# Three chunks of rows asked for together ahead of a weight load, their halo copies on another queue, and one product moved

## The chip, the core and the metric

The kernel runs on one core of a Trainium2 chip. A core has a matrix engine (TensorE, PE in the profile), a vector engine (VectorE, DVE), a scalar engine (ScalarE, ACT), a general engine (GpSimd, POOL) and a queue engine (SyncE, SP). Each takes its own instructions in their order; semaphores make one wait for another. Transfers (DMA) are issued by an instruction on GpSimd's or SyncE's queue and run on 16 DMA engines. SBUF is the memory on the core, PSUM the small one that matmuls write. The metric is the time of one execution in microseconds (us).

## What is computed

For `x` of 8 batches, 4224 tokens and 192 channels:

```python
w = softmax(weight)                       # 8 heads, 7 taps
x = causal depthwise convolution of x with w
theta = x @ w_theta                       # 192 x 192
zr, zi = x * cos(theta), x * sin(theta)
y = w_tok_r @ zr + w_tok_i @ zi           # over tokens, each w_tok 4224 x 4224
u = x + y
out = u + relu(u @ w_ch)                  # 192 x 192
```

Nearly all of the work is in the two token mixes, which are matmuls of 4224 x 4224 by 4224 x 1536.

## The kernel before

**Tiles and steps.** The tokens are cut into 33 *chunks* of 128 (four runs of 32 tokens each, `token`, L140). For each chunk the convolution, the transposes, the *channel mix* with `w_theta` and the products with cos and sin give the right sides z; sums and differences of them serve a scheme in which two output tiles of 128 tokens take seven products for each chunk instead of eight. A *step* (class `Step`) computes such a pair of output tiles over the chunks that are active; there are 58 steps. A *product* is two matmuls (L603), one for each half of the columns, 384 wide. Steps 0 and 1 are `plain`: 8 products for each chunk, with 2 and 4 chunks, 16 and 32 products. Step 2 has 5 chunks and 35 products, step 3 has 7 chunks and 49. Counting on over steps, products 1 to 16 are step 0's, 17 to 48 step 1's, 49 to 83 step 2's, 84 to 132 step 3's.

The seven runs of a step (L507 to L513) are written "11", "S1", "S2", "S4", "S3", "12", "22". Each adds into one of the PSUM tiles c1, c2, c3 and ends by *giving* it to the partial rows `pv` (`give`, L482): a copy on ScalarE (L488) or an addition on VectorE (L490). `y` tiles come from a pool of two (L105, L597). In step 2 run "S4" ends with product 68 and gives by VectorE; run "12" opens c3 with product 74, while c1 is still in use.

**The first pass over chunks 0 to 11** is the loop at L900. Iteration i convolves chunk i (`conv`, L212, two halves; line 220 is the matmul, and each half reads 96 partitions of `xw`, first of tokens runs 0 and 1, then of 2 and 3), transposes it, and mixes chunk i-1 (`theta`, L284: eight matmuls at L150, then two Sin on ScalarE at L295; products with z at L301, sums at L310 on VectorE). In between, `between(n)` lets n products of the steps pass (`more`, L876). From iteration 4 on there are 11 products in an iteration: 2 behind the first half of the convolution, 1 behind the first channel mix, 2 behind the second half, 1 behind the second mix, and 5 more. Iteration 5 holds products 25 to 35, 6 holds 36 to 46, 7 holds 47 to 57, 8 holds 58 to 68, 9 holds 69 to 79, 10 holds 80 to 90. The results of the convolution, the mixes and the transposes share two PSUM buffers in turn (`banks`, L117).

**Events.** Each step has a list of events (`step_events`, L719) with a place between 0 and 7, a seventh of the step's products being one unit; at its place an event is written into the instruction streams. They hold the weights' transposes on VectorE (`turn`, L394, from `st` to `wt`), their sums and differences (`wsum`, L402), the weight loads of the step after the next (`load_w`, L376: four DMAs on GpSimd's queue into one of two `st` tiles, first for `w_tok_r`, "m=1", at 1.3, then for `w_tok_i`, "m=2", at 4.3) and `load_rows` of the next step at 1.6 (L443: it asks for the step's two `pv` tiles). A weight load needs the `st` tile whose last transpose has been read. Step 3's second weights are loaded in step 1 at 4.3, ahead of product 37; its transpose "22", the first that reads them, is written ahead of product 60.

**Rows.** `Chunk.__init__` (L190) fills `xw` with a chunk's rows: for each of four runs a DMA from `x` on GpSimd's queue (L207, with a cast to 16 bits), and 16 rows of *halo*, the rows before the run, copied out of the `xw` tile of the chunk before by a DMA on SyncE's queue (L198). A chunk's halo copies so need the rows of the chunk before. `xw` tiles share a pool of six buffers, tag "big", with the `pv` tiles of steps from 2 on (L192, L448). In the loop, `load_chunk(i + 3)` stands behind the second channel mix.

**What sets the order.** PE, VectorE and ScalarE take their instructions as written (`in_order`, L79). On GpSimd's queue the weight loads are chained among each other (`pool`, L94), the rows' loads are not; SyncE's DMAs are not chained. Where nothing is chained the framework orders an engine's instructions at compile time. SyncE also issues the stores of convolved rows (`store`, L263) and of partial rows at the end of a step (L616, two of 768 KB).

Of the kernel before, what the change touches and what calls it, by code (L numbers as in the profile page):

```python
# [16 lines left out]
def kernel(  # L17
# [23 lines left out]
    nc = tc.nc  # L41
# [8 lines left out]
    NQ = 4  # L50
    Q = P // NQ
    NK = S // P
    NT = S // P
    HALO = 16
    WR = Q + HALO
# [5 lines left out]
    NW = 11  # L61
# [26 lines left out]
    def dve(ins):  # L88
        return in_order("dve", ins)
# [4 lines left out]
    def pool(ins):  # L94
        return in_order("pool", ins)
# [39 lines left out]
    def channel_pieces(w):  # L135

        return ((slice(0, P), 0, w[0:P, :]), (slice(0, R), 1, w[P:D, :]),
                (slice(R, P), 2, w[0:R, :]), (slice(0, P), 3, w[R:D, :]))

    def token(k, a):  # L140

        return (a * NK + k) * Q
# [44 lines left out]
    class Chunk:  # L187


        def __init__(self, k, before=None):  # L190
            self.k = k
            self.xw = wk.tile([2 * WR, 2, B, D], F16, name="xw", tag="big", bufs=6)  # L192
            for a in range(NQ):
                h, lo = a // 2, (a % 2) * WR
                t0 = token(k, a)
                hist = self.xw[lo : lo + HALO, h, :, :]
                if before is not None:
                    nc.sync.dma_start(  # L198
                        out=hist, in_=before.xw[lo + Q : lo + Q + HALO, h, :, :]
                    )  # L200
                elif t0 == 0:
                    nc.vector.memset(hist, 0.0)
                else:
                    lo, t0 = lo - HALO, t0 - HALO
                lo += HALO
                n = (a % 2 + 1) * WR - lo
                nc.gpsimd.dma_start(  # L207
                    out=self.xw[lo : lo + n, h, :, :],
                    in_=x[:, t0 : t0 + n, :].rearrange("b s d -> s b d"),
                )  # L210

        def conv(self, j):  # L212
# [95 lines left out]
        def sum(self, o, a, b):  # L308
            z = self.z
            dve(nc.vector.tensor_tensor(  # L310
                out=z[:, o, :], in0=z[:, a, :], in1=z[:, b, :], op=ALU.subtract
            ))
# [18 lines left out]
    chunks = {}  # L331

    def load_chunk(k):
        if k < NK and k not in chunks:
            chunks[k] = Chunk(k, before=chunks[k - 1] if k % NW else None)
# [370 lines left out]
    steps = [Step(t) for t in range(NSTEP)]  # L706
# [12 lines left out]
    def step_events(t):  # L719
        found = []  # L720
        s = steps[t]
        if t + 1 < NSTEP:
            found += steps[t + 1].w_tasks()
            if not steps[t].ahead_of_single():
                found.append((1.6, steps[t + 1].load_rows))
            for i in steps[t + 1].adds:
                if (t + 1, i) != first_add:
                    found.append((2 + 2 * i, lambda i=i: steps[t + 1].load_x(i)))
                found.append((3.6 + 2 * i, lambda i=i: steps[t + 1].add_x(i)))
        here = [(r, i, which) for r in steps for i, when, which in r.ahead if when == t]  # L730
        for j, (r, i, which) in enumerate(here):
            found.append((1.5 + 1.8 * j, lambda r=r, i=i, which=which: r.add_ahead(i, which)))
        if t + 2 < NSTEP:
            nxt = steps[t + 2]
            if steps[t + 1].ahead_of_single():
                found.append((4.5, lambda: nxt.load_rows(True)))
            for m in (1, 2):
                at = 1.3 + 3 * (m - 1)
                if steps[t + 1].ahead_of_single():
                    at = (0.1, 3.1)[m - 1]  # L740
                found.append((at, lambda m=m: nxt.load_w(m)))
            if nxt.ahead_of_single():
                found += nxt.early_tasks()
        if t == NPS:
            found.append((5.5, lambda: chunks[EARLY].plain_sums()))
        if t == NPS + 1:
            for k in range(EARLY + 1):
                found.append((1.2 + 0.6 * k, lambda k=k: chunks[k].sum(T3, Z22, Z12)))
        if t == start[NW - 1] + 2:
            found.append((3, lambda: steps[first_add[0]].load_x(first_add[1], True)))  # L750
        for j, k in enumerate(LATER):
            for w in range(2):
                if start[k] == t + 1:
                    found.append(((2.1 if start[k] == start[NW - 1] else 1.3) + 0.02 * j + 0.01 * w,
                                  lambda k=k, w=w: chunks[k].sums(w)))
        if t == NU - 2:
            def load_wch():
                dve(nc.vector.memset(wch[:, 1:3, :], 0.0))
                for rows, i, part_w in channel_pieces(moe_w_ch):
                    pool(nc.gpsimd.dma_start(out=wch[rows, i, :], in_=part_w))  # L760
            found.append((3, load_wch))
        for at, f in outputs:
            begin = at - sum(s.time for s in steps[:t])
            if 0 <= begin < steps[t].time:
                found.append((7 * begin / steps[t].time, f))
        if t >= NU - 2:
            new = [k for k in range(NK) if start[k] == t + 2 and k >= NW]
            for k in new:
                found.append((4.5, lambda k=k: load_chunk(k)))
            places = (  # L770
                (.1, .1, 1.1, 2.75, 3.05, 3.6, 3.65, 3.9, 4.1),
                (2.1, 2.1, 3.55, 4.6, 5.0, 5.5, 5.55, 5.8, 6.0),
            )
            new = [k for k in range(NK) if start[k] == t + 1 and k >= NW]
            for k, pos in zip(new, places):

                def add(at, j, k):
                    def go():
                        if j == 0:
                            chunks[k].todo = chunks[k].tasks()  # L780
                        next(chunks[k].todo)()
                    found.append((at, go))
                if not s.pair and start[k] >= NSTEP - NU and pos is places[1]:
                    pos = pos[:-2] + (7.0, 7.01)
                for j, p in enumerate(pos):
                    add(p, j, k)
        return found
# [12 lines left out]
    for a in range(2):  # L800
        nc.gpsimd.affine_select(
            out=sel, in_=sel, pattern=[[1, Q - 1 + 2 * WR]], channel_multiplier=-1,
# [4 lines left out]
    for a, lo in ((0, True), (1, False)):  # L807
        nc.gpsimd.affine_select(
            out=block[:, a : a + 1], in_=block[:, a : a + 1], pattern=[[0, 1]],
# [7 lines left out]
    def idle(n):  # L817
# [7 lines left out]
        out=wmax, in_=wsb, axis=mybir.AxisListType.X, op=ALU.max  # L825
    ))
    dve(nc.vector.tensor_tensor(
        out=wsb, in0=wsb, in1=wmax[:, :].unsqueeze(2).to_broadcast([P, H, KS]),
# [6 lines left out]
        out=wsum, in_=wsb, axis=mybir.AxisListType.X, op=ALU.add  # L835
# [5 lines left out]
        out=wdiag, in0=wsb[0:KS, :, :],  # L841
# [4 lines left out]
        out=wcol, in_=wdiag, axis=mybir.AxisListType.X, op=ALU.add  # L846
# [5 lines left out]
    for q in range(Q):  # L852
# [7 lines left out]
        out=bands, in0=bv.unsqueeze(2).to_broadcast([2 * WR, H, 2, Q]),  # L860
# [39 lines left out]
    for i in range(1, NW + 2):  # L900
        ch = chunks.get(i) if i < NW else None
        old = chunks[i - 1] if i <= NW else None

        def between(n):
            left = more(n)
            if i < 3:
                idle(min(left, 2) if i == 1 else 0)

        if ch:
            ch.conv(0)  # L910
        between(2)
        if old:
            old.theta(0)
        ready[0] = i - 2
        between(1)
        if ch:
            ch.conv(1)
        between(2)
        if old:
            old.theta(1)  # L920
        if i in (1, 3):
            for name in ("11", "21"):
                steps[i // 2].turn(name)
        if i + 3 < NW:
            load_chunk(i + 3)
        between(1)
        if i == 1:
            for first in (Z11, Z21):
                old.product(first, slice(0, 1))
        if ch:  # L930
            ch.transpose()
        if i == 1:
            for first in (Z11, Z21):
                old.product(first, slice(1, 2))
        elif old:
            old.product(Z11)
        between(2)
        if i > 1 and old:
            old.product(Z21)
        if i in (1, 3):  # L940
            for name in ("12", "22"):
                steps[i // 2].turn(name)
        if i == EARLY:
            for k in range(EARLY):
                chunks[k].plain_sums()
        between(1)
        summed = old and NPS < start[i - 1] and i - 1 not in LATER
        if summed:
            old.sums(0)
        between(1)  # L950
        if summed:
            old.sums(1)
        between(1)
# [34 lines left out]
```

## Time and profile before

| What | us |
|---|---|
| median of three runs (lowest, highest) | 1431.65 (1431.12, 1433.92) |
| the profiled execution | 1430.95 |
| its span | 1429.2 |
| PE busy in the span | 1408.4 |
| VectorE busy | 973.2 |
| GpSimd busy | 435.3 |
| ScalarE busy | 312.0 |
| from 54 to 70 us (16 us): VectorE, ScalarE busy | 15.33, 15.59 |

The profile is of one execution. Its times count from the span's start. A *timeline* line gives start, duration, engine, line of the code, operation, output<-inputs, shapes, and in brackets how long the engine was idle before and which instruction or transfer released it; `x4` merges four neighbours. The *waits* list sums such idle time. The *chain* follows the work that ended last back from the end. A transfer has an issue (an instruction on its queue) and a landing, which the trace records too. The releaser of a wait is inferred from semaphore events, and a wait for several is put down to the one that came last. The granted clock of TensorE was 0.999 of full speed.

### The profile page before, as it was taken

How to read it: one execution, taken by the hardware profiler on the slowest of the kernel's cores; microseconds unless marked ns; L12 is line 12 of the kernel's file. 1: busy time of each engine (PE TensorE's matmuls, PEld its weight loads, DVE VectorE, ACT ScalarE, POOL GpSimd, SP SyncE). 2: the span in 40 equal slices, each digit the busy share in tenths (PEclk: the TensorE clock that was granted, in tenths of full speed). 3: DMA queues.
4: the chain of work that ended last, by engine and by line, in shares of the span. 5: the costliest groups of instructions: out<-in, count | busy, mean ns of one | idle time of the engine just before them, and what ended most of it. 6: DMA issues, size and time to landing. Idle time of an engine off the chain costs nothing.

```text
span 1429.2 us, 23781 instructions
## 1 busy us (share of the span) xinstructions
PE 1408.4 (99%) x9829; PEld 889.5 (62%) x9829; DVE 973.2 (68%) x1047; ACT 312.0 (22%) x377; POOL 435.3 (30%) x655
## 2 busy tenths in 40 slices
PE   8899999999999999999999999999999999999997
PEld 5566666666666666666666666666566666666665
DVE  6884654545458787766665657877777677767686
ACT  5951111011134253000000004435100110010134
POOL 8521221111323322532333343233324123213110
PEclk9999999999999999999999999999999999999999
DMA  9975765564699999898899889999999999999784
GB/s 190 250 174 111 148 146 109 121 134 95 160 227 221 244 217 257 197 262 173 237 229 235 226 157 244 230 200 245 272 206 211 215 210 215 203 200 198 167 219 134
DMA packets 272046, 282.00 MB, mean 197 GB/s; under 512 B 106688, under 2 KB 240192, under 8 KB 271936
## 3 DMA queue, kind: packets, MB, share of 16 engines
q0 software_dynamic: 162464, 92.15, 49.0%
q1 hardware_dynamic: 71840, 178.88, 35.4%
q10 hardware_dynamic: 37632, 9.44, 4.3%
q8 instruction: 77, 1.26, 0.4%
q14 instruction: 33, 0.27, 0.1%
HBM read 245.49 MB, written 108.13 MB: 247 GB/s over the span
## 4 chain that ended last, share of the span: by engine, by line
PE 88%; DMA 5%; DVE 4%; ACT 1%; issue 1%; POOL 1%; SPq 0%; DVEq 0%; ACTq 0%; POOLq 0%
PE y L603 80%; PE v L150 5%; DMA st<-in_moe_w_tok_i_dram 2%; DMA st<-in_moe_w_tok_r_dram 1%; PE tp L174 1%; DMA xw<-in_x_dram 1%; PE pc L220 1%; DVE wt L396 1%; DVE pv L490 1%; ACT z L295 1%; POOL st L383 1%; DVE z L310 0%; DVE z L301 0%; DMA xs<-z 0%; DVE pv L652 0%
## 5 line engine op out<-in xcount | busy, mean ns | idle before, releaser
L603 PE MATMUL y<-z,wt 128*128 128x384 f16 x7652 | 1278.2, 326 | 2.1 <-DVE pv L490 1.0
L603 PEld LDWEIGHTS <-wt 128*128 128x128 f16 x7652 | 741.9, 98 | 477.2 <-issue 3.6
L490 DVE TENSOR_TENSOR pv<-y,pv 128x768 f32<-128x768 f32 x315 | 300.8, 955 | 320.5 <-PE y L603 274.9
L396 DVE STREAM_TRANSPOSE wt<-st 128x1408 f16<-128x1408 f16 (+7 forms) x224 | 327.7, 1466 | 44.2 <-PE y L603 36.2
L383 POOL DMA_DIRECT2D st<-in_moe_w_tok_r_dram x232 | 132.7, 578 | 457.9 <-DVE wt L396 450.9
L383 POOL DMA_DIRECT2D st<-in_moe_w_tok_i_dram x232 | 132.7, 579 | 402.6 <-DVE wt L396 390.3
L408 DVE TENSOR_TENSOR wt<-wt 128x1408 f16<-128x1408 f16 (+6 forms) x208 | 173.6, 835 | 41.8 <-PE y L603 39.4
L160 ACT ACTIVATE z<-pc 128x768 f16<-128x768 f32 (+1 forms) x62 | 47.5, 803 | 385.4 <-PE pc L220 381.1
L160 ACT ACTIVATE ub<-pv 128x768 f16<-128x768 f32 (+1 forms) x66 | 51.5, 821 | 338.7 <-DVE pv L490 336.9
L488 ACT ACTIVATE pv<-y 128x768 f32<-128x768 f32 x66 | 53.7, 814 | 278.5 <-PE y L603 278.5
L150 PEld LDWEIGHTS <-uT 128*128 128x128 f16 x1056 | 90.5, 98 | 22.9 <-issue 5.6
L468 POOL TENSOR_TENSOR pv<-pv,xr 128x1536 f32<-128x1536 f32 x24 | 74.5, 3104 | 66.1 <-issue 26.8
L207 POOL DMA_DIRECT2D xw<-in_x_dram x132 | 76.4, 585 | 28.8 <-DMA st<-in_moe_w_tok_r_dram 7.1
L652 DVE SCALAR_TENSOR_TENSOR pv<-v,pv 128x768 f32<-128x768 f32 (+1 forms) x67 | 63.0, 942 | 25.2 <-PE v L150 24.7
L310 DVE TENSOR_TENSOR z<-z 128x768 f16<-128x768 f16 x132 | 71.2, 553 | 2.3
L295 ACT ACTIVATE z<-v,half_pi 128x768 f16<-128x768 f32 x66 | 59.6, 903 | 56.2 <-PE v L150 55.5
L160 ACT ACTIVATE uT<-tp 128x1536 f16<-128x1536 f16 (+1 forms) x47 | 56.7, 1208 | 47.7 <-PE tp L174 47.7
L301 DVE TENSOR_TENSOR z<-z 128x1536 f16<-128x1536 f16 (+1 forms) x68 | 60.6, 926 | 5.1 <-ACT z L295 5.1
L150 PE MATMUL v<-wth,uT 128*128 128x192 f16 x528 | 54.4, 246 | 2.7 <-ACT z L295 2.1
L150 PE MATMUL v<-wch,uT 128*128 128x192 f16 x528 | 54.4, 246 | 0.8 <-DVE pv L652 0.5
L295 ACT ACTIVATE z<-v 128x768 f16<-128x768 f32 x66 | 53.2, 807 | 0.0
L220 PE MATMUL pc<-xw,bands 96*64 96x192 f16 x512 | 30.1, 250 | 4.1 <-DMA st<-in_moe_w_tok_r_dram 2.2
(48 smaller groups left out, 152.0 us busy)
## 6 DMA issues: line engine op xcount, KB each, us to landing
part<-pv SPq DMA_DIRECT2D x79, 768.0 KB, 4.3
pv<-part SPq DMA_DIRECT2D x79, 768.0 KB, 6.3
out_dram<-pv SPq DMA_DIRECT2D x65, 384.0 KB, 4.3
st<-in_moe_w_tok_r_dram POOLq DMA_DIRECT2D x136, 176.0 KB, 5.9
st<-in_moe_w_tok_i_dram POOLq DMA_DIRECT2D x136, 176.0 KB, 5.2
xs<-z SPq DMA_DIRECT2D x132, 96.0 KB, 5.2
xw<-in_x_dram POOLq DMA_DIRECT2D x121, 96.0 KB, 6.0
xr<-xs SPq DMA_DIRECT2D x24, 384.0 KB, 4.1
```

Source lines behind the costliest of these rows:

```text
L150: pe(nc.tensor.matmul(v[:, k, b * D : (b + 1) * D], lhsT=tT[:, 3 * k + b + i, :], rhs=w[:, 2 * b + i, :], start=(i == 0), stop=(i == 1),))
L160: act(nc.scalar.activation(out=out, in_=in_, func=AT.Copy))
L207: nc.gpsimd.dma_start(out=self.xw[lo : lo + n, h, :, :], in_=x[:, t0 : t0 + n, :].rearrange("b s d -> s b d"),)
L295: act(nc.scalar.activation(**args))
L310: dve(nc.vector.tensor_tensor(out=z[:, o, :], in0=z[:, a, :], in1=z[:, b, :], op=ALU.subtract))
L383: pool(nc.gpsimd.dma_start(out=st[a * Q : (a + 1) * Q, 0:nb, :, 0:n] .rearrange("i r bt s -> i (r bt) s"), in_=w[self.tbs[0] * P : (self.t ...
L396: dve(nc.vector.transpose(self.w[name][:, 0 : self.n, :, :], self.st[int(name[1])][:, int(name[0]) - 1, :, 0 : self.n * Q] .rearrange("p b ...
L408: dve(nc.vector.tensor_tensor(out=self.w[name][:, 0 : self.n, :, :], in0=self.w[a][:, 0 : self.n, :, :], in1=self.w[b][:, 0 : self.n, :, : ...
L468: ins = pool(nc.gpsimd.tensor_tensor(out=self.pv[i], in0=self.pv[i], in1=self.xr[i], op=ALU.add))
L490: dve(nc.vector.tensor_tensor(out=o, in0=yv, in1=o, op=ALU.add))
L603: pe(nc.tensor.matmul(y[cn][:, q, 0:BH], lhsT=self.w[wn][:, c, :, :].rearrange("p bt i -> p (bt i)"), rhs=chunks[k].z[:, zn, q * BH : (q + ...
L652: dve(nc.vector.scalar_tensor_tensor(out=ub[:, ks, :], in0=v[:, ks, :], scalar=0.0, in1=ub[:, ks, :], op0=ALU.max, op1=ALU.add,))
```

## The change

Four edits.

- `load_rows` of step 2 (an event of step 1) moves from 1.6 to 6.9, the end of step 1. In the first pass it only asks for buffers.
- The rows of chunks 8, 9 and 10 are all asked for in iteration 5, behind its second channel mix; before, those of chunk 9 came in iteration 6 and those of chunk 10 in iteration 7. By that they come ahead of step 3's second weights (written in iteration 6) on GpSimd's queue.
- The halo copies of chunks 9 and 10 (four each) leave SyncE's queue and are issued on GpSimd's, behind the rows of all three chunks. Chunk 8's stay on SyncE.
- From iteration 3 on, three products instead of two stand between the second half of the convolution and the second channel mix, and one instead of two between the product with cos (`Z11`) and that with sin (`Z21`). An iteration has 11 products as before.

```diff
@@ Chunk.__init__
                 if before is not None:
-                    nc.sync.dma_start(
-                        out=hist, in_=before.xw[lo + Q : lo + Q + HALO, h, :, :]
-                    )
+                    if not 8 < k < NW:
+                        nc.sync.dma_start(
+                            out=hist, in_=before.xw[lo + Q : lo + Q + HALO, h, :, :]
+                        )
@@ Chunk
+        def halos(self, before):
+            for a in range(NQ):
+                h, lo = a // 2, (a % 2) * WR
+                nc.gpsimd.dma_start(
+                    out=self.xw[lo : lo + HALO, h, :, :],
+                    in_=before.xw[lo + Q : lo + Q + HALO, h, :, :],
+                )
@@ step_events
-                found.append((1.6, steps[t + 1].load_rows))
+                found.append((6.9 if t == 1 else 1.6, steps[t + 1].load_rows))
@@ the loop over i
-        between(2)
+        between(2 if i < 3 else 3)
         if old:
             old.theta(1)
...
-        if i + 3 < NW:
+        if i < 5:
             load_chunk(i + 3)
+        if i == 5:
+            for k in range(8, NW):
+                load_chunk(k)
+            for k in range(9, NW):
+                chunks[k].halos(chunks[k - 1])
...
             old.product(Z11)
-        between(2)
+        between(2 if i < 3 else 1)
```

## The prediction

> **What bounds the kernel now.** I read the page first, then the chain in order of time, PE's waits, and the timelines of PE, VectorE, GpSimd and SyncE around the longest wait.
>
> ```profile
> span 1429.2 us, 23781 instructions
> PE 1408.4 (99%) x9829; PEld 889.5 (62%) x9829; DVE 973.2 (68%) x1047; ACT 312.0 (22%) x377; POOL 435.3 (30%) x655
> ```
>
> PE is idle for 20.8 us of the span. In the chain, the piece that starts at 89.31 is 322.42 us of matmuls without a break, and PE's waits from 90 to the end sum to 2.2 us. So the end moves with whatever moves PE at about 89 us, one for one. PE's waits from 36 to 90 us are (columns: total, times, longest):
>
> ```profile
> PE pc L220 <- DMA st<-in_moe_w_tok_r_dram: 2.2, 1, 2.2
> PE v L150 <- ACT z L295: 1.1, 6, 0.3
> PE y L603 <- ACT pv L488: 1.0, 2, 0.7
> PE pc L220 <- DMA xw<-in_x_dram: 0.8, 1, 0.8
> PE tp L174 <- ACT z L160: 0.2, 1, 0.2
> ```
>
> 5.3 us in all is the most that this change can reach. The wait of 2.2 us is in iteration 9, whose first convolution reads chunk 9 (start, duration, then the idle time before):
>
> ```profile
> 69.57 0.27 PE L220 MATMUL pc<-xw,bands 96*64 96x192 f16 x1
> 72.01 0.49 PE L220 MATMUL pc<-xw,bands 96*64 96x192 f16 x7 [2.17 <-DMA st<-in_moe_w_tok_r_dram]
> 75.61 0.82 PE L150 MATMUL v<-wth,uT 128*128 128x192 f16 x8 [0.16 <-ACT z L295]
> 76.26 0.49 PE L603 MATMUL y<-z,wt 128*128 128x384 f16 x2
> ```
>
> The releaser named is a weight load, but line 224 needs no weights: it needs chunk 9's rows and halo copies. GpSimd issues the rows (L207) behind step 3's second weights (L383, tok_i), which wait for a transpose on VectorE; SyncE issues the copies (L198) behind two partial-row stores (L616):
>
> ```profile
> 47.79 1.72 POOL L207 DMA_DIRECT2D xw<-in_x_dram  x3
> 49.86 0.58 POOL L207 DMA_DIRECT2D xw<-in_x_dram  x1 [0.35 <-DMA xw<-in_x_dram]
> 53.28 2.29 POOL L383 DMA_DIRECT2D st<-in_moe_w_tok_i_dram  x4 [2.84 <-DVE wt L396]
> 55.55 3.42 POOL L207 DMA_DIRECT2D xw<-in_x_dram  x6
> 60.00 1.27 POOL L207 DMA_DIRECT2D xw<-in_x_dram  x2 [1.02 <-DMA st<-in_moe_w_tok_i_dram]
> ```
> ```profile
> 56.74 2.44 SPq L616 DMA_DIRECT2D part<-pv  x2
> 61.68 5.48 SPq L198 DMA_DIRECT2D xw<-xw  x4
> ```
>
> Chunk 9's rows landed by 65.65; its last two copies landed at 71.52 and 71.88. PE goes on at 72.01, so the copies are what is late.
>
> The fourth engine to read is VectorE:
>
> ```profile
> 52.14 0.84 DVE L396 STREAM_TRANSPOSE wt<-st 128x640 f16<-128x640 f16 x1
> 54.46 0.49 DVE L408 TENSOR_TENSOR wt<-wt 128x640 f16<-128x640 f16 x1 [1.48 <-PE y L603]
> 67.71 1.10 DVE L396 STREAM_TRANSPOSE wt<-st 128x896 f16<-128x896 f16 x1
> 74.69 0.95 DVE L490 TENSOR_TENSOR pv<-y,pv 128x768 f32<-128x768 f32 x1
> 75.56 1.10 DVE L396 STREAM_TRANSPOSE wt<-st 128x896 f16<-128x896 f16 x1
> ```
>
> From 54.46 to 81.92 it has no idle time over 0.04 us: it is behind its orders. The add at 74.69 (L490) belongs to product 68, the end of run S4, which PE finished at about 69.6. Product 74 opens run "12" with a new y tile; there are two, c1 is still in use, so it needs the one that this add frees at 75.64. PE came to product 74 at 76.26, 0.6 us later. **Without its stall PE would run into this add.** No wait shows it yet.
>
> **The change, part by part.** One product is two matmuls of 0.163 us (375 took 61.12), so 0.33 us.
>
> *The product moved ahead of the second mix.* The number of products in an iteration stays 11. The mix waits 0.16 us for the Sin of the first mix (six such waits sum to 1.1), and 0.33 us covers that. The order on ScalarE changes too: in iteration 5 the copy of product 30 (46.08, 0.81) came behind two Sin instructions (start to start 1.49), and product 33 waited 0.74 for it; now it comes ahead of them. Gained between 40.14 (a wait on chunk 5's data that swallows what was gained earlier) and 54.4 are 0.16 + 0.74 + 0.16 = 1.06 us. ScalarE is busy 13.64 of 16 us from 38 to 54, so less may come; bounds 0 to 1.06. This matters at one place: VectorE's weight difference at 54.46 waits 1.48 us for PE to finish with the tile that it overwrites. Its unbroken stretch can so begin 1.1 us sooner (at most 1.48).
>
> *Rows of chunks 8 to 10 together.* They leave at iteration 5, and the pv tiles of step 2, which held two of six buffers from 1.6 of step 1, are asked for at its end. They are first written by product 53's copy, when the buffers of chunks 5 and 6 are free: cost nothing. Chunk 8's four issues stay. GpSimd keeps eight transfers in flight: chunk 10's last two rows left at 60.00 and 60.69, 0.28 after the eighth transfers before them landed (59.72, 60.41). By that, chunk 9's rows follow the landings of step 3's first weights (50.49 to 52.62), the last at 52.9; chunk 10's follow those of chunk 8's (53.50 to 55.00), the last at 55.3.
>
> *The eight halo copies on GpSimd.* Eight issues of 0.58 us. Chunk 9's follow the landings of chunk 9's rows (5.1 to 5.7 us after issue, as chunk 8's took): the last at about 58.9. Chunk 10's follow chunk 10's rows: the last at 61.3, and GpSimd is free at 61.9. The copies land 4.5 to 7.9 us after issue, as SyncE's eight did: chunk 9's by 63.4 to 66.8. PE will want them at 69.57 - 1.06, about 68.5. The 2.17 us go.
>
> *Step 3's second weights.* These pay. They were issued from 53.28, landing by 60.41. Now they stand behind eight rows and eight copies, and the eight-in-flight rule ties the last to the landing of chunk 9's last copy: issued at 63.7 to 67.1. From issue to landing weights took between 4.0 us (in the quiet at 76.95) and 8.2 (at 63.65 to 65.94). So they land between 67.7 and 75.3. Nearest row: chunk 10's rows, which stood in the same queue when the two 768 KB stores took 88% of the engines (62 to 66.3), landed from 68.61 to 70.22. The weights take their place, and the stores come some 0.7 us sooner, with PE: I take **69.5**.
>
> Their reader is the transpose at 67.71, which would now be reached at 67.71 - 1.1 = 66.6. VectorE then stands 69.5 - 66.6 = 2.9 us, with the add of product 68 seven microseconds behind the transpose on the same engine, and PE behind the add.
>
> Here a rule speaks against the move to GpSimd. Its issues took 578 ns each, minimum as maximum, for 17 row issues from 34.6 to 60.7, while VectorE was busy 15.33 of 16 us from 54 to 70. The Trainium skill (SBUF — State Buffer, "SBUF: two separate sides") says that certain VectorE copies lock GpSimd out of the port through which it writes a transfer's descriptors, and that transfers issued from SyncE are immune. Had each of the eight issues to wait for one VectorE instruction of 0.95 us, the weights would be 7.6 us later. The row shows no such wait, and the stretch holds products, sums and transposes, no copies; I add nothing.
>
> **The sum.** The add of product 68 now ends at 75.64 - 1.1 + 2.9 = 77.44, and product 74 starts at 77.5. In the new order product 74 stands ahead of the second mix, so from it to the next iteration's convolution lie five more products (with itself six, 1.96), the mix 0.65 and the transposes 0.66: 3.27 us, hence 80.77. Before, the convolution started at 78.98. **Net +1.8 us.** Put generally: stall of the transpose minus 1.1. From there each order is followed as before (iteration 10's second mix is tied to Sin as it was), and PE is full.
>
> The profiled execution took 1430.95 us (span 1429.2 and 1.75 around it): 1432.75. It lies 0.70 below the median shown, so for a median I say 1433.4. That is +0.13%: within 0.2% (2.9 us), about what a measurement of this kernel can tell from no change.
>
> **Rivals.**
>
> *Weights in time (chance 0.2).* GpSimd's order may put the weights ahead of the copies, since row and copy issues are not chained to them; or everything lands sooner, by 66.6. For: GpSimd idles 2.84 us before 53.28, room for five issues. Against: it kept the written order at 29.65 and 53.28, where it stood idle for weights with free rows behind them. Then net -1.1 (at most -1.5, the whole of VectorE's wait): 1431.65 - 1.1, 1430.5 for the median.
>
> *Slower: the weights land after 70.6 (0.28).* Same mechanism, one price: every microsecond of landing is one of PE. The change is over +0.2% when the transpose stalls for more than 4.0 us. For: those in-flight ties are serial (rows, then copies, then weights), each step takes 5 to 8 us while the engines are loaded (DMA share 1.24 from 54 to 70), and the stores fall between. Against: the same bytes had all landed by 74.4 before, the first weights of step 4 included, and these now go last. Landing at 73: stall 6.4, net +5.3, 1437.0; at 75.3: 1439.3.
>
> *The full gain (0.05).* If product 74 got a tile without the add, PE would lose only its own waits, 2.17 + 1.06 and two of 0.2: net -3.6, 1428.0. Against: two y tiles (L106), and run order at L507.
>
> *The stall stays (0.03).* Copies on GpSimd land after 71: PE waits as before; about 1432 to 1434.
>
> **How the numbers follow.** Forecast with stalls of 1.1 to 4.0 us: 0.44, time 1433.4. With the rivals above: faster by over 0.2% 0.06 (the full gain and a little), slower 0.29, within 0.2% 0.65. The range takes the gain of 1.5 at its low end and a landing at 73 at its high end: 1430.0 to 1437.0.
>
> **What would show it.** Right: no wait at the first convolution of iteration 9; the four tok_i issues after 61; VectorE idle 2 to 4 us before the 128x896 transpose that stood at 67.71, named by a DMA; PE idle for several us ahead of product 74, named by L490; the first convolution of iteration 10 at about 80.8. Wrong: tok_i at 53 again, VectorE without that idle time, or product 74 not waiting on L490. The prediction fails most easily in the landing time of the weights, which decides sign and size.

## The result, and the profile after

The changed kernel took 1438.79 us (median of 6 runs, 1436.38 to 1440.28). The kernel before, measured beside it, took 1431.38 (6 runs). The ratio is 1.0047 [1.0034, 1.0059] (in brackets the 95% interval): slower by about 7 us. The forecast was 1433.4, and the range ended at 1437.0. What happened is the rival "slower", with its mechanism: the median lies between its two prices, 1437.0 for a landing at 73 and 1439.3 for 75.3.

The profiled execution after took 1440.28 us. It is the longest of the six, so it shows more of the loss than the median does. The two lines of its page that answer to those shown of before:

```profile
span 1438.6 us, 23769 instructions
PE 1409.8 (98%) x9829; PEld 889.6 (62%) x9829; DVE 973.2 (68%) x1047; ACT 312.0 (22%) x377; POOL 439.0 (31%) x663
```

The span is 9.4 us longer. The work of VectorE and ScalarE is the same to the tenth, and GpSimd has eight issues more (x663 for x655) for 3.7 us. PE's idle time went from 20.8 to 28.8 us, and its busy time, for the same 9829 matmuls, up by 1.4. So 8.0 us are waits, and 1.4 are matmuls that took longer. Line numbers after are nine higher than before from the convolution on (L220 is L229, the product L603 is L612); the rows' loads are L208, and L216 is the new copies on GpSimd.

PE's two longest waits from 36 to 100 us after (columns: total, times, longest; four more, all on ScalarE, sum to 2.2):

```profile
PE y L612 <- DVE z L319: 6.4, 1, 6.4
PE y L612 <- DVE pv L499: 3.3, 1, 3.3
```

No line of the six names chunk 9's data any more: the 2.17 us are gone. Two waits of products on VectorE stand in their place. PE's timeline after shows where (start, duration, idle time before it):

```profile
69.11 0.53 PE L229 MATMUL pc<-xw,bands 96*64 96x192 f16 x8
69.58 0.82 PE L612 MATMUL y<-z,wt 128*128 128x384 f16 x4
70.31 0.83 PE L150 MATMUL v<-wth,uT 128*128 128x192 f16 x8
77.58 0.80 PE L612 MATMUL y<-z,wt 128*128 128x384 f16 x2 [6.43 <-DVE z L319]
...
83.84 0.80 PE L612 MATMUL y<-z,wt 128*128 128x384 f16 x2 [3.30 <-DVE pv L499]
84.44 1.49 PE L150 MATMUL v<-wth,uT 128*128 128x192 f16 x8
85.72 0.85 PE L612 MATMUL y<-z,wt 128*128 128x384 f16 x2
86.36 1.19 PE L174 MATMUL tp<-ident,z 128*128 128x128 f16 x12
87.38 1.46 PE L612 MATMUL y<-z,wt 128*128 128x384 f16 x8
```

The first row is chunk 9's convolution, without a wait. The wait at 83.84 is the predicted one: product 74, behind the add of product 68. The one at 77.58 is product 71, in run S3, which reads a sum that VectorE writes just behind the late transpose; it is the same lateness of VectorE, met one run earlier. Two matmuls, which took 0.49 before, now take 0.80. The first convolution of iteration 10 starts at 88.77 (78.98 before).

VectorE after:

```profile
67.30 0.62 DVE L417 TENSOR_TENSOR wt<-wt 128x896 f16<-128x896 f16 x1
75.97 1.11 DVE L405 STREAM_TRANSPOSE wt<-st 128x896 f16<-128x896 f16 x1 [8.05 <-DMA st<-in_moe_w_tok_i_dram]
...
82.84 0.95 DVE L499 TENSOR_TENSOR pv<-y,pv 128x768 f32<-128x768 f32 x1
```

This is the source. The transpose of step 3's second weights stands 8.05 us for their landing, and the add of product 68 (at 74.69 before) stands behind it in order. Both are as predicted; the size is not. GpSimd after:

```profile
54.80 2.29 POOL L208 DMA_DIRECT2D xw<-in_x_dram  x4 [0.18 <-issue]
57.43 0.52 POOL L216 DMA_DIRECT2D xw<-xw  x1 [0.34 <-DMA xw<-in_x_dram]
58.47 0.50 POOL L216 DMA_DIRECT2D xw<-xw  x1 [0.53 <-DMA xw<-in_x_dram]
60.80 1.48 POOL L216 DMA_DIRECT2D xw<-xw  x3 [1.83 <-DMA xw<-in_x_dram]
64.91 0.49 POOL L216 DMA_DIRECT2D xw<-xw  x1 [2.62 <-DMA xw<-in_x_dram]
68.05 1.07 POOL L216 DMA_DIRECT2D xw<-xw  x2 [2.66 <-DMA xw<-in_x_dram]
69.19 2.32 POOL L392 DMA_DIRECT2D st<-in_moe_w_tok_i_dram  x4
```

Chunk 10's rows leave from 54.80 on, the last at 56.5 (55.3 was expected). Then the copies (L216) wait five times, 8.0 us in all, each for an older transfer to land: by the order of the issues three times for rows of chunk 9 (2.7 us) and twice for rows of chunk 10 (5.3). Chunk 10's rows landed at 61.52, 64.63, 67.77 and 68.36, and copies left at 64.91 and 68.05, 0.28 behind the second and the third of these. The weights, last in order, left from 69.19 and landed from 72.71 to 75.85. VectorE went on at 75.97.

The rows took 6.7 to 11.8 us; the DMA queues suggest why. From 58 to 61 us GpSimd's queue (q0) moved 932 packets in the trace, 311 per us, and SyncE's (q1) 0.39 MB. SyncE's two 768 KB stores left at 56.74 and 57.3 and landed at 64.34 and 66.72; most of their bytes moved from 61 to 66 us, when the queues of the kernel after were (packets, MB, share of the engines):

```profile
q1 hardware_dynamic: 373, 1.66, 85.0%
q0 software_dynamic: 311, 0.24, 20.8%
```

The stores' queue (q1) held 85% of the engines, and q0 fell to 62 packets per us.

**The account**, at the first convolution of iteration 10: the stall of 8.05; VectorE reached the transpose 0.13 later than before (its instruction ahead of it started at 67.30, for 67.17); and 4.93 us instead of 3.27 from product 74 to the convolution, 1.66 more. That makes 9.84; the timelines show 88.77 - 78.98 = 9.79. The span grew by 9.4, so 0.4 came back later. For the 1.66, the windows of the kernel after (stretch, its length, the busy time of PE, PEld, VectorE, ScalarE and GpSimd with the number of instructions in brackets, then the granted clock, the DMA share and GB/s):

```profile
70.00:72.00 2.00, 1.14 (x11) 0.70 (x10) 0.00 (x0) 1.77 (x4) 2.00 (x4) 1.00 0.91 107
72.00:74.00 2.00, 0.00 (x0) 0.00 (x0) 0.00 (x0) 0.78 (x2) 1.79 (x4) 0.86 1.09 113
74.00:76.00 2.00, 0.00 (x0) 0.00 (x0) 0.03 (x1) 0.00 (x0) 0.00 (x0) 0.50 1.20 144
...
84.00:86.00 2.00, 2.00 (x11) 1.52 (x10) 2.00 (x3) 0.04 (x1) 0.90 (x2) 0.50 0.00 0
86.00:88.00 2.00, 2.00 (x18) 1.57 (x17) 1.28 (x3) 1.92 (x3) 1.39 (x3) 0.73 0.88 102
```

While PE waited, its granted clock fell to 0.50, and it stayed there until about 87, three microseconds after product 74 had set PE going for good.

### The profile page after: what moved, and what is told of

The parts are those of the page before. It is cut to its first block, busy times and chain, and to the rows that moved or that the text cites. A ratio compares the mean times of both kernels' runs of the same rounds, so it can differ in the third digit from the quotient of the medians.

```text
span 1438.6 us, 23769 instructions
## 1 busy us (share of the span) xinstructions
PE 1409.8 (98%) x9829; PEld 889.6 (62%) x9829; DVE 973.2 (68%) x1047; ACT 312.0 (22%) x377; POOL 439.0 (31%) x663
## 4 chain that ended last, share of the span: by engine, by line
PE 91%; DMA 4%; DVE 1%; ACT 1%; POOL 1%; issue 1%; DVEq 0%; ACTq 0%; POOLq 0%; SPq 0%
PE y L612 83%; PE v L150 5%; DMA xw<-in_x_dram 3%; PE tp L174 1%; PE pc L229 1%; ACT z L304 1%; POOL xw L208 1%; DVE pv L499 0%; DMA xs<-z 0%; DMA st<-in_moe_w_tok_r_dram 0%; DMA st<-in_moe_w_tok_i_dram 0%; POOL st L392 0%; ACT uT L160 0%; DVE wt L405 0%; DVE pv L661 0%
## 5 line engine op out<-in xcount | busy, mean ns | idle before, releaser
L612 PE MATMUL y<-z,wt 128*128 128x384 f16 x7652 | 1279.7, 326 | 11.6 <-DVE z L319 6.4
L612 PEld LDWEIGHTS <-wt 128*128 128x128 f16 x7652 | 742.2, 98 | 487.4 <-issue 13.5
L477 POOL TENSOR_TENSOR pv<-pv,xr 128x1536 f32<-128x1536 f32 x24 | 74.5, 3106 | 66.8 <-issue 26.3
L208 POOL DMA_DIRECT2D xw<-in_x_dram x132 | 76.3, 585 | 28.1 <-issue 6.4
L304 ACT ACTIVATE z<-v,half_pi 128x768 f16<-128x768 f32 x66 | 60.0, 910 | 61.9 <-PE v L150 61.2
L229 PE MATMUL pc<-xw,bands 96*64 96x192 f16 x512 | 30.5, 252 | 3.7 <-DMA xw<-in_x_dram 1.3
```

The source lines that it names most:

```text
L208: nc.gpsimd.dma_start(out=self.xw[lo : lo + n, h, :, :], in_=x[:, t0 : t0 + n, :].rearrange("b s d -> s b d"),)
L304: act(nc.scalar.activation(**args))
L477: ins = pool(nc.gpsimd.tensor_tensor(out=self.pv[i], in0=self.pv[i], in1=self.xr[i], op=ALU.add))
L612: pe(nc.tensor.matmul(y[cn][:, q, 0:BH], lhsT=self.w[wn][:, c, :, :].rearrange("p bt i -> p (bt i)"), rhs=chunks[k].z[:, zn, q * BH : (q + ...
```

## The experiments

My theory after the result: the eight copies on GpSimd's queue, in front of the weights, make the weights wait for chunk 10's rows; VectorE's written order carries that to the add, and the add to PE; the lower clock adds to it. The rivals: the loss is in the products' new order; or the early rows alone fill the DMA engines; or the clock makes most of it. Each ratio below compares with the kernel before, measured beside the run (its medians there were 1431.5 to 1432.6).

**Halo copies back on SyncE.** The change without its third edit:

```diff
-                    if not 8 < k < NW:
-                        nc.sync.dma_start(
+                    nc.sync.dma_start(
...
-            for k in range(9, NW):
-                chunks[k].halos(chunks[k - 1])
```

> The change without its third part: the halo copies of chunks 9 and 10 stay on SyncE, rows and products as changed. Theory (the late landing of step 3's second weights stops VectorE, and PE behind it): the weights now wait on GpSimd only for chunk 10's rows, are issued by about 61 and land at 66 to 69, where VectorE comes to their transpose at about 67.9. Its idle time falls from 8.05 us to 0 to 1.5, and the time to 1430 to 1434. Rival one (the moved product is what costs): 1437 to 1440, as changed. Rival two (twelve rows asked for together slow every transfer): the weights land after 72 all the same, 1435 to 1439.

Measured: 1434.05, ratio 1.0011 [1.0002, 1.002], at the very end of what was expected. GpSimd's timeline of this kernel, then VectorE's:

```profile
56.54 2.29 POOL L391 DMA_DIRECT2D st<-in_moe_w_tok_i_dram  x4
```
```profile
70.11 1.10 DVE L404 STREAM_TRANSPOSE wt<-st 128x896 f16<-128x896 f16 x1
```

The weights leave 12.6 us sooner and land by 65.44, and the transpose carries no bracket: VectorE no longer waits for them. Most of the loss is gone with the copies, though the early rows are still there. PE's waits from 36 to 100 us name what comes next:

```profile
PE pc L228 <- DMA xw<-xw: 2.9, 2, 2.5
PE y L611 <- DVE pv L498: 2.1, 2, 1.9
```

At chunk 9 only 0.41 us are left of the first line; its 2.47 belong to chunk 5's copies at 42 us, which no edit touches. The wait at this place differs between executions of one kernel too (0.78 and 1.34 in the two profiles of the kernel before). Here it makes VectorE later as well: its weight difference waits 2.4 us for PE. Product 74 waits 1.86 us for the add although nothing stalls VectorE: this is the bound that the prediction had set 0.6 us behind the old wait. With chunk 9's wait gone, VectorE is next.

**Weights ahead of the copies.** All copies still on GpSimd, but written an iteration later, behind the weights:

```diff
-            for k in range(9, NW):
-                chunks[k].halos(chunks[k - 1])
+        if i == 6:
+            for k in range(9, NW):
+                chunks[k].halos(chunks[k - 1])
```

> The change with its eight halo copies still on GpSimd, but written in iteration 6, behind step 3's second weights. Theory: the weights no longer wait for the landing of chunk 10's rows (67.8, 68.4 in the changed kernel); VectorE idles under 2 us before their transpose, 1430 to 1434. The price moves to the copies: they are issued after the weights, land near 70, and PE may wait up to 2 us in iteration 9, where it would meet VectorE's add anyway. Rival (the halo copies on GpSimd cost by themselves, wherever they stand): 1436 or more.

Measured: 1432.75, ratio 1.0005 [0.9994, 1.0017]. VectorE's timeline and PE's waits of this kernel:

```profile
69.69 1.11 DVE L405 STREAM_TRANSPOSE wt<-st 128x896 f16<-128x896 f16 x1 [1.37 <-DMA st<-in_moe_w_tok_i_dram]
```
```profile
PE pc L229 <- DMA xw<-xw: 2.0, 2, 1.3
PE y L612 <- DVE pv L499: 1.8, 2, 1.5
```

With the order turned round, the stall falls from 8.05 to 1.37, and what is late now are the copies (landed 69.73 to 71.79; chunk 9's convolution waits 1.27 and 0.69).

**Only the products' new order.** The kernel before with the fourth edit alone.

> The kernel before with the fourth edit alone: three products ahead of the second channel mix from iteration 3 on, transfers as before. Theory (all of the loss comes from the transfers' order, none from the product): within 1.5 us of the kernel before, the waits of PE on Sin gone (1.1 us down to under 0.5), the wait on chunk 9's copies and VectorE's addition as the next bound left. Rival (the product ahead of the mix is what costs, since product 74 now holds up the mix): 2 us or more above the kernel before.

Measured: 1431.67, ratio 1.0000 [0.9988, 1.0011]. The order of the products neither loses nor gains more than 1.7 us by this interval. It also shows why the 1.06 us that I had counted did not reach VectorE. Its weight difference in this kernel:

```profile
54.23 0.49 DVE L408 TENSOR_TENSOR wt<-wt 128x640 f16<-128x640 f16 x1 [1.51 <-PE y L603]
```

It still waits 1.51 us for PE and starts 0.23 sooner than before, not 1.06. In the trace after, iteration 5 takes 6.68 us from convolution to convolution instead of 8.14 (before, counted from 39.87, which leaves out the 0.78 that its first convolution waited), but it starts 0.87 later (at 40.74), and iteration 6 takes 7.12 instead of 6.99.

**The change without the products' new order.**

> The changed kernel without its fourth edit: products placed as before, transfers as changed. Theory: VectorE waits for step 3's second weights as in the changed kernel, landing between 71 and 76, time 1435 to 1441. Rival (product order makes the loss): 1430 to 1433.

Measured: 1436.48 (5 runs), ratio 1.0043 [1.003, 1.0055]. The loss stays without the fourth edit. How it comes about is less clean in this kernel's profile: 2.27 us at 41 to 43 went to chunk 5's copies, the clock then fell to 0.61 from 44 to 48, and VectorE's weight difference started at 58.57, 4.11 later than before, so that its transpose stalled only 0.81 us for weights that landed at 72.58. Those 4.11 us are not from the transfers that the change moves, so this run confirms the sign by its time and not the path. Why the other four runs, without a profile, lie as high is open.

**VectorE's order changed.** The changed kernel with the late transpose (step 3's "22", the one that stalls) and its two sums written later, behind work that needs no weights. In step 3 their places were 2.2, 3.05 and 3.3; the other places of the list stay:

```diff
+            if self.t == 3:
+                return [
...
+                    (2.05, lambda: self.wsum("S3")), (4.0, lambda: self.turn("22")),
+                    (4.05, lambda: self.wsum("S1")), (4.1, lambda: self.wsum("S2")),
...
```

> The changed kernel, all DMAs as they are, with three VectorE instructions of step 3 (transpose 22 and the sums S1, S2 that read it) written behind the addition of product 68 instead of ahead of it. Theory (the loss is what stands behind the transpose on VectorE, the weights themselves are not needed yet): the addition and the sum that product 71 waits for no longer wait for the landing at 75.9; the waits of 6.4 and 3.3 us on PE go, and a shorter one is left at product 79, whose run needs an addition behind the transpose: near 80 instead of 78.7. Time 1432 to 1435. Rival (PE needs the weights, or waits for transfers): 1437 to 1440.

Measured: 1430.79, ratio 0.9989 [0.9981, 0.9998], better than I had expected. GpSimd is nearly as late as after: the weights were issued from 66.82 and landed by 73.17, 6.8 us behind the place where VectorE would have come to their transpose in the order of after (66.39, when the sum ahead of it was done). VectorE's timeline is now, with a row of PE behind it:

```profile
71.25 0.95 DVE L506 TENSOR_TENSOR pv<-y,pv 128x768 f32<-128x768 f32 x1
73.29 1.11 DVE L405 STREAM_TRANSPOSE wt<-st 128x896 f16<-128x896 f16 x1 [1.10 <-DMA st<-in_moe_w_tok_i_dram]
```
```profile
77.64 0.48 PE L619 MATMUL y<-z,wt 128*128 128x384 f16 x2 [2.27 <-DVE pv L506]
```

The add stands ahead of the transpose, and product 74 waits 0.69 us. The late weights are not free here: product 79 (the row of PE) waits 2.27 us for an add behind the transpose, as expected, and the granted clock was 0.55 and 0.59 in the two stretches of 2 us from 78. But most of what they cost after was the cost of what was queued behind the instruction that waits for them.

**The wait filled.** The changed kernel with 40 matmuls of 384 columns ahead of product 71, which compute nothing of the output and only keep PE busy:

```diff
+        if i == 9:
+            fill = banks("fill")
+            for _ in range(40):
+                pe(nc.tensor.matmul(fill[:, 0, 0 : 2 * D], lhsT=ident, ...
```

> The changed kernel with 40 extra matmuls of 384 columns (about 6.5 us, into a PSUM tile that nobody reads) on PE ahead of product 71, in the place of its wait of 6.4 us. They compute nothing of the output. Theory A (the lower granted clock after the wait, 0.54 from 77.5 to 88 us, is a cost of its own, about 1.7 us up to iteration 10): the clock stays near 1 and the time falls by 1.5 to 2.5 us against the changed kernel, to 1436 to 1437.5. Theory B (the clock costs nothing, since PE waits there anyway): 1438 to 1440.

Measured: 1435.71 (12 runs, 1433.40 to 1441.76), ratio 1.0031 [1.0016, 1.0047]. The runs lie in two groups, 1433.4 to 1436.2 and 1438.3 to 1441.8, and in the profiled one (1433.95) the weights landed at 71.19 and the stall was 3.33. Its time is therefore no measure of the clock alone. The trace is:

```profile
77.50:88.00 10.50, 10.50 (x104) 7.15 (x102) 7.96 (x10) 7.40 (x10) 2.28 (x4) 1.00 0.76 160
```

The clock is 1.00 (the value behind the five engines), and from product 74 to the convolution of iteration 10 it takes 3.37 us: the order's 3.27 again, not 4.93. So the clock's part is read as 1.6 us in the traces; by the times it stays inconclusive.

**The late transpose with other transfers.** Copies on SyncE, and the late transpose:

> Two of the edits tried so far together: halo copies of chunks 9 and 10 on SyncE as before, and transpose 22, S1, S2 of step 3 behind the addition of product 68. Theory: the weights land before VectorE wants them, and the addition comes some 2 us sooner since three instructions of 1.1, 0.6 and 0.6 us have left its way, so neither stops PE; left is the wait on chunk 9's copies (0.5 to 2.5 us): 1428.5 to 1431. Rival (e4's gain came from the copies on GpSimd and is lost with them): 1431.5 or more.

Measured: 1432.19, ratio 1.0003 [0.9994, 1.0012]; a miss, inside the range of the rival. Chunk 9's convolution waits 0.53 and 1.20 us for the copies, and VectorE waits for a store that stands on the same SyncE queue:

```profile
74.05 1.22 DVE L318 TENSOR_TENSOR z<-z 128x768 f16<-128x768 f16 x2 [1.86 <-DMA xs<-z]
```

The kernel before with the new products' order and the late transpose, no transfer moved:

> The kernel before with the moved product and with transpose 22, S1, S2 of step 3 behind the addition of product 68; transfers all as before. Theory: the wait of 2.2 us on chunk 9's copies stays, the addition behind it is no bound any more: 1429.5 to 1431.5, 0 to 2 us under the kernel before. If it is as fast as the version with the early rows, the early rows are worth nothing; if 1.5 us slower, they are worth the wait that they take away.

Measured: 1432.6, ratio 1.0012 [1.0003, 1.0021]; a miss too. PE's timeline keeps the old wait:

```profile
72.18 0.24 PE L220 MATMUL pc<-xw,bands 96*64 96x192 f16 x1 [2.71 <-DMA st<-in_moe_w_tok_r_dram]
```

This kernel and the one with all four edits and the late transpose differ in the first three edits alone. Each was measured against the kernel before, 1.0012 and 0.9989, which is some 3 us between them (1.8 by their medians). The two intervals do not overlap, so the early rows and the copies on GpSimd do bring something, once VectorE's order allows for late weights.

**Chunk 10 behind the weights.** Rows of 8 and 9 and chunk 9's copies in iteration 5, chunk 10's rows and copies in iteration 6, behind the weights:

```diff
-            for k in range(8, NW):
+            for k in (8, 9):
                 load_chunk(k)
-            for k in range(9, NW):
-                chunks[k].halos(chunks[k - 1])
+            chunks[9].halos(chunks[8])
+        if i == 6:
+            load_chunk(10)
+            chunks[10].halos(chunks[9])
```

> The changed kernel with chunk 10 taken out of the early block: in iteration 5 the rows of chunks 8 and 9 and chunk 9's four copies, then step 3's second weights, then chunk 10's rows and copies, all on GpSimd. Theory (the weights were late because chunk 10's rows, caught behind the two 768 KB stores, had to land before its copies could be issued in front of the weights): the weights are issued by about 61 and land before 69.5; VectorE idles under 1.6 us, PE has chunk 9's copies in time; 1430 to 1433. Rival (any block of copies on GpSimd in front of the weights costs the same): 1435 or more.

Measured: 1431.43, ratio 0.9998 [0.9989, 1.0007]. VectorE and PE of this kernel:

```profile
67.17 1.11 DVE L405 STREAM_TRANSPOSE wt<-st 128x896 f16<-128x896 f16 x1 [0.76 <-DMA st<-in_moe_w_tok_i_dram]
```
```profile
75.04 0.80 PE L612 MATMUL y<-z,wt 128*128 128x384 f16 x2 [3.62 <-DVE pv L499]
```

Chunk 9's copies are still in front of the weights, and the stall is 0.76. What cost 7 us was thus chunk 10: four rows and four copies that PE needs only an iteration later. PE does not wait for chunk 9, but in the place of the old 2.17 it loses 3.62 us to the add.

The same with the late transpose:

> The order of transfers of the run with chunk 10 behind the weights, and transpose 22, S1, S2 of step 3 behind the addition of product 68. Theory: neither chunk 9's copies nor the weights stop anything, and the addition of product 68 comes about 2 us sooner: 1428.5 to 1430.5, under the kernel before. Rival (something else bounds iterations 8 to 10, such as ScalarE): 1431 or more.

Measured: 1430.48, ratio 0.9977 [0.9964, 0.999]. And with chunk 7's sums written later as well (`LATER = [LATER[0] - 2, LATER[0] - 1] + LATER`):

> The run before, with the four sums of chunk 7 (2.2 us on VectorE, first read in step 4) also written later, with those of chunk 8. Theory: VectorE's lag at product 68 falls by another 2.2 us, PE finds its tile free at products 74 and 79: another 0.5 to 1.5 us less than the run before it. Rival (the lag was gone already): the same within 0.5 us.

Measured: 1428.53, ratio 0.9972 [0.9963, 0.9981], faster than both kernels, by 0.28% than before. The ratio is of 11 of its 12 runs, 1426.87 to 1431.03; the twelfth took 1473.99. VectorE's and PE's rows of this kernel:

```profile
68.73 0.95 DVE L506 TENSOR_TENSOR pv<-y,pv 128x768 f32<-128x768 f32 x1
```
```profile
PE y L619 <- DVE pv L506: 1.7, 1, 1.7
```

The add comes 6 us sooner than before, between 70 and 80 us PE is busy 10.00 of 10.00, and the wait of 1.7 lies at 94. Whether the later sums add to the step before is not settled: the two intervals overlap. The first edit, the later request for step 2's rows, was never run alone; it stands in this kernel too, so by itself it does not make the loss.

**The kernel before once more.**

> The kernel before, unchanged, for a second profile. Theory: its VectorE stretch from about 54.5 to 82 without idle time, and the wait of 1 to 3 us on chunk 9's copies, stand again; landing times of single transfers between 40 and 70 us shift by 1 to 3 us from execution to execution.

Measured: 1430.59. Chunk 9's convolution waits as it did (PE's timeline of this execution):

```profile
71.10 0.24 PE L220 MATMUL pc<-xw,bands 96*64 96x192 f16 x1 [1.91 <-DMA xw<-xw]
72.06 0.49 PE L220 MATMUL pc<-xw,bands 96*64 96x192 f16 x7 [0.71 <-DMA st<-in_moe_w_tok_r_dram]
```

The weight difference starts at 54.01 and the add of product 68 at 74.24, within half a microsecond of the first profile. The wait and what lies behind it belong to the kernel, not to one execution.

## Why the prediction was wrong

**Right.** GpSimd kept the written order. VectorE stood at the transpose for the weights, PE at product 74 for the add, and the transpose's stall came through to the next convolution one for one. The eight-in-flight rule held (0.28 us from landing to issue). No issue waited for VectorE: copies took 0.49 to 0.52 us each. The rival's point of decision, a stall of more than 4.0 us, was passed.

**Right by luck.** Chunk 9's wait went, as step "the eight halo copies" said. But that step had the copies landing by 63.4 to 66.8, 4.5 to 7.9 us after issue. They took 7.8 to 11.1 us and landed from 68.53 to 69.1, and PE came to them at 69.11. Had it come at about 68.5, as the step says, it would have waited for them by some 0.6 us.

**The step that failed: "Chunk 10's follow chunk 10's rows: the last at 61.3, and GpSimd is free at 61.9."** Measured: the last copy left at 68.64, and GpSimd was free for the weights at 69.19, 7.3 us later. Of this, 1.2 us are the rows' own issue. The rest is their landing: I gave chunk 10's rows the 5.1 to 5.7 us that chunk 8's had taken, issued from 47.8 on, and they took 6.7 to 11.8. The profile before had a nearer row: the rows of chunks 9 and 10, issued there from 55.55 on, took 5.7 to 10.8. The landings of the last rows fell into the stretch of the stores, which I had applied only to the weights. The bounds for the weights' issue (63.7 to 67.1) did come from the copies' landings, but the copies were tied to rows that I had landing too early, and they too took longer than I had. By the eight-in-flight rule chunk 9's copies alone, landing until 69.1, would have held the last weight until about 69.4.

That isn't the whole of it. The landing of the rows varies from one profile to another with the same order of transfers: the last of chunk 10's rows landed at 68.36 (after), 65.83 (late transpose), 61.59 (filled wait) and 61.78 (without the products' order). In the last two GpSimd was free about when I had said: the weights left from 62.82 and 62.91, and landed by 71.19 and 72.58 all the same, since then they met the stores themselves. All four are later than the 69.5 that I chose. It was taken from chunk 10's rows in the kernel before, first and last of which landed at 68.61 and 70.22, while the row for weights under the stores was 8.2 us from issue to landing (single ones 7.6 to 8.8; the shortest in that profile was 3.6, at 53.28, and not 4.0). With my own earliest issue of the last weight, 63.7, that row gives 71.9, and its stall of 5.3 us lies on the other side of the 4.0.

**The gain of 1.1 us** never reached VectorE: 0.23 in the kernel with the products' order alone, and -0.13 after. The changed order of ScalarE moved the wait from iteration 5 into iterations 4 and 6 (0.86 and 0.24 us after). After, VectorE was held by something else too: its transpose at 48.03 (46.52 before) began when step 2's second weights had landed, at about 47.95, and the weight difference followed at 54.59 without a wait for PE. My lower bound of 0 was near the value.

**Not in the sum at all: the clock.** It cost 1.66 us in the profiled execution, and I had it at nothing. The wait of 2.17 in the profile before had left the clock at 1.00, and I had no row with a longer one there.

That the stores delay the rows is read from the queues' packets and the landings, and is not shown by a kernel in which the stores alone were changed. One profile fits it: without the products' order the first store left at 60.92 instead of 56.74, chunk 10's rows took 3.7 to 4.7 us, and the weights, issued from 62.91 on, took 7.0 to 7.9. That the transfers in front of the weights are the cause, and VectorE's order the carrier, is shown from both sides: by taking chunk 10 or the copies away, and by moving the transpose.

## What to carry to other kernels

An issue that waits, on a queue that works in order, delays everything written behind it until the slowest landing it is tied to; price the landings by the load of the stretch into which they are moved, not of that from which the row was taken. Before moving a transfer ahead of another, ask which of the two is wanted first: here half of what went ahead was wanted an iteration later. And where an engine must wait for late data, look at what is queued behind the waiting instruction: three instructions written later on VectorE took the loss away with the order of the transfers as it was.

## What the runs showed of the hardware that was not expected

The granted clock. After PE's last matmul ahead of product 71, at 71.14, it was 1.00 until about 73.4 (0.86 over 72 to 74, if it fell in one step to 0.50); it came back at about 87.1 (0.73 over 86 to 88), 3.2 us after product 74.

The Trainium skill ("TensorE: Matmul & The Clock Gate", section "Part 1: The HAM clock gate (the "warmup" mystery)") gives half rate after at least one idle window of about 3.4 us, and full rate after about 3.4 us of sustained work. The return after 3.2 us agrees. The fall does not: it came 2.3 us after the last matmul, sooner than a whole window of 3.4, and here the measurement decides. Nor is the length of the wait all. 2.17 us at a stretch (before) left the clock at 1.00. With the late transpose and no transfer moved, PE was idle for 3.03 of the 10 us from 70 to 80, 2.71 at a stretch, and the clock was 1.00 there. With the products' order alone it was idle for 1.51 of these 10 us, 1.18 and 0.91 at a stretch from 69.4 on, and the clock was 0.83. With the copies on SyncE 2.47 us at a stretch, ending at 42.15, were followed by a clock of 0.50 from 42 to 44. What tells these apart stays open.

While two stores of 768 KB on another engine's queue moved most of their bytes, GpSimd's queue fell from 311 to 62 packets per us for five microseconds; the same is in the trace before (365 per us from 58 to 62, 70 from 62 to 66.3).
